# A mixture-of-experts tail: one scatter-add for the shared slot, an earlier bound of G, a later half of the second G

## The chip, the cores and the metric

The kernel runs on one core of a Trainium2 chip. The metric is the device time of one execution, in microseconds (us); several executions are run and their median is given. The engines' names are those of the profile: PE (TensorE matmul; PEld its weight loads), DVE (VectorE), ACT (ScalarE), POOL (GpSimd), SP (SyncE, which issues most DMAs). L789 means line 789 of the kernel before.

## The reference

Local-window attention feeds a soft mixture of experts, and that feeds a top-2 mixture of 8 experts. The change lies in the last part, of which this is the core:

```python
top2 = np.argpartition(-noisy_logits, 2, axis=1)[:, :2]
...
out = np.zeros((N, D), dtype=np.float32)          # N = 1536, D = 512, E = 8, F = 1024
for e in range(E):
    for k in range(2):
        mask = top2[:, k] == e
        h = np.maximum(x[mask] @ w1[e], 0.0)
        out[mask] += top2_w[mask, k, None] * (h @ w2[e])
```

Here `x` is the output of the soft mixture, `x = c @ slot_out`, with only 32 columns in `c`. So the kernel never forms `x`: for each expert it computes G = slot_out @ w1 once, and a row's `x @ w1` is its row of `c` times G.

## The kernel before

**Slots.** The 3072 (token, expert) pairs are sorted into slots of 128 rows: three slots for each expert (0 to 23), and one shared slot, number 24, that takes rows of up to four experts in four groups of 32. For slot n the kernel gathers the rows of `c` (`slot_a`, an indirect DMA issued by POOL, six slots ahead), transposes them (`slot_t`), computes h in 8 matmuls (`slot_h`; ACT writes the relu's high half, DVE the low half in `slot_l`), and then y in three times 8 matmuls of 512 columns (`slot_y`: high x high, high x low weight, low x high). ACT scales y into `ys`, and POOL adds the 128 rows to `out` in HBM with an indirect DMA that accumulates (`add_out`). Adds of one expert's three slots may overlap, since no token stands twice in them. Every other add waits until the adds before it have landed.

**Ranks.** Rank r is the preparation of expert r, laid out over the slots of the experts before it. Its steps are: `g_mm` (G into PSUM, tile `pg`), `w_abs` (ACT, maxima of w2), `w_scale_a` (L757, DVE: maximum of these into column 0 of `wx`), `g_scale_a` (L785, ACT: maximum of G into `gm`), `g_bound` (L789, DVE: a bound from `gm` into column 1 of `wx`), `scale_b` (two one-column spreads on PE, L722, one for each column of `wx`, then powers of two on DVE, `pow2`, L732 to L735), `g_hi`, `g_lo`, `w_hi`, `w_lo` (splits into two fp16 halves) and `g_put` (G to its place). In the kernel before `g_bound` is called inside `scale_b`.

**Order.** From L677 on, PE, DVE and ACT take their instructions in the order in which the program writes them, and POOL's adds and gathers are kept in order as well. The loop at L1363 writes a slot as: `do(n,"0")`, 8 matmuls of y(n), h(n+1), `do(n,"l")`, low half of h(n+1), transpose of n+2, `do(n,"a")`, 16 matmuls of y(n), `do(n,"p")`, ys(n), adds, `do(n,"b")`. A rank step at place k falls on slot (BASE[r]+k)/4, quarter "0", "a", "p" or "b" by the remainder. So step 3 of rank 2 falls on (2,"b") and step 5 on (3,"a"). The shared slot's own steps stand in the list `SHARE`.

**The shared slot's end.** One token can have both of its rows in slot 24. An indirect add with one row twice would lose one of them. So `tok` has two last columns, for the first and the second choice, `rows()` (L1178) makes two columns of row numbers from them, and `Shared.add` runs twice over the same `ys`, each time with the other choice's rows sent to padding rows behind the output.

**Start of this part.** K0 and K1 are ranks 0 and 1. `direct` (L1079) makes the first two transposed row tables by matmuls with one-hot matrices instead of gathers. At L1107 the first half of K1's G stands between the first `direct` and h of slot 0.

Of the kernel before, what the change touches and what calls it, by code (L numbers as in the profile page):

```python
# [8 lines left out]
F32 = mybir.dt.float32  # L9
F16 = mybir.dt.float16  # L10
# [9 lines left out]
NTOK = 1536  # L20
# [18 lines left out]
         (21, "a", "mm", 6), (21, "a", "mm", 7), (21, "a", "end"), (21, "p", "add", NOWN), (21, "p", "add", NSLOT)]  # L39
BASE = [0, 0, 8, 19, 30, 41, 51, 62]  # L40
# [16 lines left out]
def emit(tc, d, near=True, stop=None):  # L57
    nc = tc.nc
    es = ExitStack()
    with es:  # L60
# [14 lines left out]

        c32 = cst.tile([128, 393 + NSLOT], F32, name="c32")

        def cut32(a, n):
            return c32[:, a:a + n]

        ident, sel4, blkm, iof = cut32(0, 128), cut32(128, 128), cut32(256, 4), cut32(260, 32)
        padrow, ovth, below = cut32(292, 1), cut32(293, 72).rearrange("p (e k) -> p e k", e=8), cut32(365, 8)
        sltm, quarter, pads = cut32(373, NOV), cut32(391, 1), cut32(392, NSLOT + 1)
        out = d["out"]
# [653 lines left out]
        class Rank:  # L738
# [26 lines left out]
            def scale_b(self):  # L765
                self.g_bound()
                (self.sw, self.iw), (self.sg, self.ig) = pow2(self.wx, "w")
# [221 lines left out]
        class Shared:  # L989
# [22 lines left out]
            def h(self):  # L1012
                room = ring(2).bitcast(F16)
                self.hh = room[:, 0:2048].rearrange("p (a f r) -> p a f r", a=2, f=8)
                self.ys = room[:, 2048:3072].bitcast(F32)
                self.phs = []
                for q in range(2):
                    ph = ps_h.tile([128, 4, 128], F32, name="h")
                    for i in range(4):
                        f = 4 * q + i  # L1020
                        for g in range(4):
                            a = 32 * g
                            nc.tensor.matmul(ph[:, i, a:a + 32], self.gq[:, g, 128 * f:128 * f + 128], self.ct[:, a:a + 32],  # L1023
                                             start=True, stop=True)
                    nc.scalar.activation(self.hh[:, 0, 4 * q:4 * q + 4], ph, AF.Relu)
                    self.phs.append(ph)
                slot_l(self.hh, self.phs)
# [22 lines left out]

            def add(self, c):
                pool_q.indirect_dma_start(out=out, out_offset=bass.IndirectOffsetOnAxis(ap=sidx[:, c:c + 1], axis=0),
                                             in_=self.ys, in_offset=None, compute_op=ALU.add)
# [25 lines left out]
        def direct(z):  # L1079
            pct = pm_([128, 128])  # L1080
            for t in range(NT):
                nc.tensor.matmul(pct, c16[:, t].rearrange("p a s -> p (a s)"), z[t // 6][:, :, t % 6], start=(t == 0),
                                 stop=(t == NT - 1))
            return pct
# [21 lines left out]
        K0.w_hi(1)  # L1106
        K1.g_mm((0, 1))  # L1107
        h0 = slot_h(0, t0, scratch([128, 2, 8, 128], F16))
        pct1 = direct(z1)
        for q in range(2, 4):  # L1110
            K0.w_hi(q)
# [16 lines left out]
        gidx = cs2.tile([128, NSLOT], I32, name="gidx")  # L1128
        sidx = cs2.tile([128, NSLOT + 1], I32, name="sidx")
        adds, late, sent = [], [], []  # L1130
# [44 lines left out]
        og = scratch([128, 2, NSLOT, 24], F16)  # L1175
        tok, pad = scratch([128, NSLOT + 1], F32), scratch([128, NSLOT + 1], F32)

        def rows():  # L1178

            ttt(tok[:, NSLOT - 1:NSLOT], tok[:, NSLOT - 1:NSLOT], tok[:, NSLOT:], ALU.subtract)  # L1180
            nc.vector.scalar_tensor_tensor(pad, tok, 0.0, pads, ALU.is_equal, ALU.mult)
            nc.vector.scalar_tensor_tensor(sidx, tok, -1.0, pad, ALU.add, ALU.add)

# [57 lines left out]
        def rank_steps(r):  # L1241


            def k(place, nm, *a):
                j, q = divmod(BASE[r] + place, 4) if isinstance(place, int) else (OWN * r - 3 + int(place[0]), place[1])
                at(j, "0apb"[q] if isinstance(q, int) else q, lambda: getattr(raw[r], nm)(*a))
# [11 lines left out]
            if r == 1:  # L1258
                k("1l", "w_scale_b")
                k("1l", "g_put", 1)  # L1260
            else:
                for q in range(4):
                    k((-1, 0, 1, 1)[q], "w_abs", q)
                k(2, "w_scale_a")
                k(5, "scale_b")
                k(5, "g_hi")
# [49 lines left out]
        nc.vector.tensor_scalar(gidx, pls[:, 0:NSLOT], -1.0, 0.0, ALU.add, ALU.max)  # L1316
        nc.vector.tensor_copy(tok, pls)  # L1317
        K0.w_lo(0)
        next(y0)
# [37 lines left out]
        do(1, "p")  # L1357
        list(y1)
        rows()
        slot_a(AHEAD + 1)  # L1360
# [153 lines left out]
def host(inputs, near=True):  # L1514
# [10 lines left out]
    crel[:, 167:] = -8.0 * 2.0 ** -(2.0 * np.arange(4) + i[:, None] // 64 + 1)  # L1525
    c32 = np.zeros((128, 393 + NSLOT), f32)
    c32[:, 0:128] = np.eye(128)
# [8 lines left out]

    c32[:, 392:] = i[:, None] + NTOK + 1 + 128 * (np.arange(NSLOT + 1) % OWN)
    c16 = np.zeros((128, K16W), f16)
# [46 lines left out]
```

## Time and profile before

| what | us |
|---|---|
| median of 3 runs (lowest, highest) | 358.52 (357.67, 359.04) |
| the profiled execution | 358.8 |
| its span, first to last instruction | 357.0 |
| around the span | 1.8 |
| PE busy (share of the span) | 326.3 (91%) |
| DVE, ACT, POOL busy | 226.8, 210.4, 126.9 |

A row of the timeline gives start and duration in us, the engine, the line, the operation, output and inputs, shape and count, and in brackets how long the engine had been idle before it and what ended that. Several like instructions in a row are merged into one row with their count. The granted clock of TensorE is 1.00 at 2.4 GHz and 0.50 at 1.2 GHz.

### The profile page before, as it was taken

To read this page: it belongs to the slowest core of one execution; us is meant where nothing else is said; L and a number is where in the kernel's file an instruction comes from. 1 tells how busy PE (TensorE), PEld (TensorE's weight loads), DVE (VectorE), ACT (ScalarE), POOL (GpSimd) and SP (SyncE) were. 2 spreads that over 40 slices of the span, in tenths; PEclk is the share of its full clock that TensorE was granted. 3 is DMA by queue.
4 is the path that set the end of the run, shared out by engine and by line. 5 is a ranking of instruction groups with operands and counts; after the bars stand their busy time and mean duration, and the time that the engine had idled before them with its cause. 6 is when DMAs were issued, how large, how long until landed. Compare 5 with 4: busy or idle time off the path is not lost. (4 is left out here: it accounts for less than half of the span.)

```text
span 357.0 us, 7647 instructions
## 1 busy us (share of the span) xinstructions
PE 326.3 (91%) x2666; PEld 187.0 (52%) x2666; DVE 226.8 (64%) x856; ACT 210.4 (59%) x494; POOL 126.9 (36%) x184
## 2 busy tenths in 40 slices
PE   6999999999998999978989799999996999999950
PEld 3677876787775443434554345444443544554420
DVE  7797858778746300186979783879495667977100
ACT  4787765778652211196629676767785686476210
POOL 6365544446310001200442543355326142611350
PEclk9999999999999999998989899999999899999995
DMA  7998888898999999999989999995847443233352
GB/s 198 303 327 269 292 321 266 261 328 277 272 335 382 397 394 393 395 402 397 388 198 344 315 380 349 372 347 132 258 64 180 124 57 45 34 44 47 46 79 30
DMA packets 44876, 89.61 MB, mean 251 GB/s; under 512 B 3248, under 2 KB 11952, under 8 KB 44832
## 3 DMA queue, kind: packets, MB, share of 16 engines
q1 hardware_dynamic: 40352, 81.49, 65.6%
q0 software_dynamic: 4480, 7.57, 14.0%
q8 instruction: 23, 0.38, 0.4%
q14 instruction: 21, 0.17, 0.2%
HBM read 77.91 MB, written 11.14 MB: 249 GB/s over the span
## 5 line engine op out<-in xcount | busy, mean ns | idle before, releaser
L1143 PE MATMUL y<-w2hl,hh 128*128 128x512 f16 x552 | 128.8, 388 | 0.0
L1143 PEld LDWEIGHTS <-hh 128*128 128x128 f16 x552 | 53.1, 100 | 63.4 <-issue 7.8
L225 ACT ACTIVATE Tt<-Tt,nm 128x167 f32<-128x167 f32 x96 | 40.7, 426 | 21.4 <-DVE nm L223 17.4
L237 POOL TENSOR_TENSOR Pb<-Tt,r 128x318 f32<-128x318 f32 x48 | 34.5, 719 | 45.2 <-DVE r L233 16.3
L1074 DVE SCALAR_TENSOR_TENSOR hh<-h,hh 128x512 f16<-128x512 f32 x46 | 29.5, 684 | 23.2 <-ACT hh L1066 23.1
L1152 POOL DMA_INDIRECT out_y<-ys,sidx x16 | 26.0, 1622 | 47.3 <-ACT ys L1149 46.4
L217 PE MATMUL s<-kx,qd 128*128 128x167 f32 x192 | 36.7, 332 | 3.4 <-DVE kx L203 1.7
L684 POOL DMA_INDIRECT cT<-ctab,gidx x23 | 28.0, 1215 | 23.3 <-DVE w2hl L1317 16.6
L217 PEld LDWEIGHTS s<-kx,qd 128*128 128x128 f32 x192 | 30.8, 210 | 7.0 <-issue 3.5
L223 DVE CUSTOM_DVE_ANT_0 Tt<-s,bias 128x167 f32<-128x167 f32 x96 | 27.8, 323 | 6.5 <-PE s L217 3.9
L248 PE MATMUL pt<-c,Pb 128*128 128x128 f32 x176 | 28.9, 285 | 0.6 <-POOL Pb L237 0.6
L1066 ACT ACTIVATE hh<-h 128x512 f16<-128x512 f32 x46 | 24.8, 592 | 7.4 <-PE h L1065 6.8
L268 PE MATMUL px<-PT,vt 128*64 128x128 f32 x352 | 28.9, 285 | 0.0
L1152 POOL DMA_INDIRECT out_y<-c,sidx x8 | 13.9, 1742 | 40.4 <-ACT hh L1066 12.9
L248 PEld LDWEIGHTS pt<-c,Pb 128*128 128x128 f32 x176 | 18.9, 140 | 8.3 <-issue 4.5
L268 PEld LDWEIGHTS px<-PT,vt 128*64 128x64 f32 x352 | 18.3, 136 | 7.8 <-issue 4.3
L1149 ACT ACTIVATE ys<-y,gsc 128x512 f32<-128x512 f32 x16 | 10.9, 682 | 19.2 <-PE y L1143 19.2
L250 ACT ACTIVATE PT<-pt 128x512 f32<-128x512 f32 (+1 forms) x32 | 17.8, 558 | 4.8 <-PE pt L248 3.5
L773 DVE SCALAR_TENSOR_TENSOR w2hl<-w2hl,pmw 128x1024 f16<-128x1024 f32 x16 | 20.1, 1278 | 0.1
L773 DVE SCALAR_TENSOR_TENSOR w2hl<-w,pmw,w2hl 128x1024 f16<-128x1024 f32 x16 | 20.0, 1276 | 0.1
L750 ACT ACTIVATE w2hl<-w 128x1024 f16<-128x1024 f32 x16 | 16.8, 1049 | 4.1 <-DVE w2hl L773 2.9
L770 ACT ACTIVATE w2hl<-w,pmw 128x1024 f16<-128x1024 f32 x16 | 17.6, 1143 | 1.5 <-DVE pmw L734 1.5
(295 smaller groups left out, 513.9 us busy)
## 6 DMA issues: line engine op xcount, KB each, us to landing
w<-in_w1a SPq DMA_DIRECT2D x16, 512.0 KB, 6.9
w<-in_w2a SPq DMA_DIRECT2D x16, 512.0 KB, 6.4
w<-in_w1a SPq DMA_DIRECT2D x8, 1024.0 KB, 8.9
w<-in_w2a SPq DMA_DIRECT2D x8, 1024.0 KB, 11.8
w<-in_w1b SPq DMA_DIRECT2D x8, 1024.0 KB, 13.6
w<-in_w2b SPq DMA_DIRECT2D x8, 1024.0 KB, 9.3
w2hl<-in_w1b SPq DMA_DIRECT2D x8, 1024.0 KB, 17.3
w2hl<-in_w2b SPq DMA_DIRECT2D x8, 1024.0 KB, 17.4
```

The costliest lines, as they stand in the source:

```text
L217: nc.tensor.matmul(s[:, t, :], qv[:, p, t, :], kx[T % 2][:, p, t, :], start=True, stop=True)
L223: nc.vector.tensor_tensor_reduce(Tt[:, t], s[:, t], bias[:, p, v], -0.125, 1e30, ALU.add, ALU.min, nm[:, t:t + 1])
L225: nc.scalar.activation(Tt[:, t], Tt[:, t], AF.Exp, bias=nm[:, t:t + 1], scale=-1.0, accum_out=st[:, t:t + 1])
L237: nc.gpsimd.tensor_tensor(pv, Pu[:, :, 8:167], r.unsqueeze(2).to_broadcast([128, 2, 159]), ALU.mult)
L248: nc.tensor.transpose(pt[:, ch, t], Pn[:, t, 128 * ch:128 * ch + 128], ident)
L268: nc.tensor.matmul(px[64 * h:64 * h + 64, p, :], vv[:, c:c + 64], PT[:, ch, :, 64 * h:64 * h + 64], start=(ch == 0 or m == 0), stop=(ch == 1))
L684: return lambda *a, **k: tc.keep_in_program_order(getattr(nc.gpsimd, op)(*a, **k))
L773: nc.vector.scalar_tensor_tensor(w2hl[:, self.r, 1, 2 * q:2 * q + 2], self.quarter(q), self.sw, w2hl[:, self.r, 0, 2 * q:2 * q + 2], ALU.m ...
L1066: nc.scalar.activation(hh[:, 0, 4 * q:4 * q + 4], ph, AF.Relu)
L1074: nc.vector.scalar_tensor_tensor(hh[:, 1, 4 * q:4 * q + 4], phs[q], 0.0, hh[:, 0, 4 * q:4 * q + 4], ALU.max, ALU.subtract)
L1143: nc.tensor.matmul(py, hh[:, hx, f], w2hl[:, e, wx, f], start=(n == 0), stop=(n == 23))
L1152: a = nc.gpsimd.indirect_dma_start(out=out, out_offset=bass.IndirectOffsetOnAxis(ap=sidx[:, j:j + 1], axis=0), in_=ys, in_offset=None, com ...
```

## The change

1. **Shared slot.** `rows()` compares the tokens of the shared slot's rows with each other (`twin`, 128x128, by one matmul `pl_tok` that puts the transposed token numbers into PSUM and one DVE pass) and sends one row of each pair to padding. The new `Shared.sum` multiplies `ys` by `twin` in one fp32 matmul of 512 columns, so that each row holds the sum of its token's rows, and DVE copies the result. `Shared.add` runs once.
2. **G's bound.** `g_bound` leaves `scale_b` and becomes step 3 of ranks 2 to 7, two quarters before it.
3. **Second G.** `K1.g_mm((0, 1))` moves behind h of slot 0 and the second `direct`.

```diff
-         (21, "a", "mm", 6), (21, "a", "mm", 7), (21, "a", "end"), (21, "p", "add", NOWN), (21, "p", "add", NSLOT)]
+         (21, "a", "mm", 6), (21, "a", "mm", 7), (21, "a", "end"), (21, "p", "sum"), (21, "p", "add")]
...
             def scale_b(self):
-                self.g_bound()
                 (self.sw, self.iw), (self.sg, self.ig) = pow2(self.wx, "w")
...
-                self.ys = room[:, 2048:3072].bitcast(F32)
+                self.ys, self.total = (room[:, a:a + 1024].bitcast(F32) for a in (2048, 3072))
...
-            def add(self, c):
-                pool_q.indirect_dma_start(out=out, out_offset=bass.IndirectOffsetOnAxis(ap=sidx[:, c:c + 1], axis=0),
+            def sum(self):
+
+                pz = ps_g.tile([128, 512], F32, name="pg")
+                nc.tensor.matmul(pz, twin, self.ys, start=True, stop=True)
+                self.ys = self.total
+                nc.vector.tensor_copy(self.ys, pz)
+
+            def add(self):
+                pool_q.indirect_dma_start(out=out, out_offset=bass.IndirectOffsetOnAxis(ap=sidx[:, NOWN:NSLOT], axis=0),
...
-        K1.g_mm((0, 1))
         h0 = slot_h(0, t0, scratch([128, 2, 8, 128], F16))
         pct1 = direct(z1)
+        K1.g_mm((0, 1))
...
-            ttt(tok[:, NSLOT - 1:NSLOT], tok[:, NSLOT - 1:NSLOT], tok[:, NSLOT:], ALU.subtract)
-            nc.vector.scalar_tensor_tensor(pad, tok, 0.0, pads, ALU.is_equal, ALU.mult)
-            nc.vector.scalar_tensor_tensor(sidx, tok, -1.0, pad, ALU.add, ALU.add)
+            both = tok[:, NOWN:NSLOT]
+            nc.vector.tensor_scalar(twin, pl_tok, both, None, ALU.is_equal)
+            nc.vector.tensor_reduce(pad[:, 0:1], twin, AX.X, ALU.add)
+            nc.vector.scalar_tensor_tensor(pad[:, 0:1], pad[:, 0:1], 1.5, tok[:, NSLOT:], ALU.is_gt, ALU.mult)
+            ttt(both, both, pad[:, 0:1], ALU.subtract)
+            nc.vector.scalar_tensor_tensor(pad, tok[:, 0:NSLOT], 0.0, pads, ALU.is_equal, ALU.mult)
+            nc.vector.scalar_tensor_tensor(sidx, tok[:, 0:NSLOT], -1.0, pad, ALU.add, ALU.add)
...
                 k(2, "w_scale_a")
+                k(3, "g_bound")
                 k(5, "scale_b")
...
         nc.vector.tensor_copy(tok, pls)
+        nc.vector.tensor_copy(tok16, pls[:, NOWN:NSLOT])
...
+        pl_tok = pm_([128, 128])
+        nc.tensor.matmul(pl_tok, tok16.to_broadcast([128, 128]), id16, start=True, stop=True)
         rows()
```

Left out are the sizes of constants and of `sidx`, and the two new tiles.

The order on DVE in slots 2 and 3, where rank 2's scale is made (`wx` the two maxima, `gm` the maximum of G, `pmw` the powers of two), before:

```order
L757 TENSOR_REDUCE wx<-wm 128x1
L773 SCALAR_TENSOR_TENSOR w2hl<-w2hl,pmw 128x1024
L1137 TENSOR_TENSOR gsc<-gate,invs 128x1
L1074 SCALAR_TENSOR_TENSOR hh<-h,hh 128x512 x2
L983 COPY ct<-m 128x128
L789 TENSOR_SCALAR wx<-gm 128x1
L732 TENSOR_REDUCE pmw<-m 128x2
```

The same place with the change:

```order
L757 TENSOR_REDUCE wx<-wm 128x1
L788 TENSOR_SCALAR wx<-gm 128x1
L772 SCALAR_TENSOR_TENSOR w2hl<-w2hl,pmw 128x1024
L1143 TENSOR_TENSOR gsc<-gate,invs 128x1
L1080 SCALAR_TENSOR_TENSOR hh<-h,hh 128x512 x2
L982 COPY ct<-m 128x128
L732 TENSOR_REDUCE pmw<-m 128x2
```

The bound moved ahead of five instructions. In rank 5 it moves ahead of the four from `gsc` to `ct` in the same way. In ranks 3, 4, 6 and 7 the order on DVE stays as it was.

The end of DVE's queue, from the shared slot's scale (`gsc`) on, before:

```order
L1046 TENSOR_TENSOR shx<-shx,invs 128x8
L1047 TENSOR_REDUCE gsc<-shx 128x1
L1048 TENSOR_TENSOR gsc<-gsc,gate 128x1
L1137 TENSOR_TENSOR gsc<-gate,invs 128x1
L1074 SCALAR_TENSOR_TENSOR hh<-h,hh 128x512 x2
```

And with the change:

```order
L1045 TENSOR_TENSOR shx<-shx,invs 128x8
L1046 TENSOR_REDUCE gsc<-shx 128x1
L1047 TENSOR_TENSOR gsc<-gsc,gate 128x1
L1055 COPY w_4137<-pg 128x512
L1143 TENSOR_TENSOR gsc<-gate,invs 128x1
L1080 SCALAR_TENSOR_TENSOR hh<-h,hh 128x512 x2
```

The copy of the sum stands ahead of the scale of slot 22 and of the low half of h of slot 23. On PE the one matmul of the sum stands between the 16 last matmuls of y(21) and the 8 first of y(22).

The end of POOL's queue (`w_...` the shared slot's rows, `c_...` and `ys` those of slots 21 to 23), before:

```order
L1152 DMA out_y<-ys,sidx 1920x512 x2
L684 DMA out_y<-w_4130,sidx 1920x512 x2
L1152 DMA out_y<-c_4411,sidx 1920x512
L1152 DMA out_y<-ys,sidx 1920x512 x2
L1391 TENSOR_LOAD regs_2433
```

And with the change:

```order
L1158 DMA out_y<-ys,sidx 1920x512 x2
L684 DMA out_y<-w_4137,sidx 1920x512
L1158 DMA out_y<-c_4420,sidx 1920x512
L1158 DMA out_y<-ys,sidx 1920x512 x2
L1407 TENSOR_LOAD regs_2433
```

One of the two adds of the shared slot is gone.

## Rows read from the trace of the kernel before

**Rows 1.** The page, part 1: busy time and share of the span.

```profile
PE 326.3 (91%) x2666; PEld 187.0 (52%) x2666; DVE 226.8 (64%) x856; ACT 210.4 (59%) x494; POOL 126.9 (36%) x184
```

**Rows 2.** Waits of PE, 185 to 345 us: total, times, longest.

```profile
PE m L722 <- DVE wx L789: 3.6, 2, 2.5
PE m L722 <- DVE wx L757: 1.9, 1, 1.9
...
```

**Rows 3.** Timeline around rank 2's spread, slots 2 and 3.

```profile
192.51 5.34 PE L1143 MATMUL y<-w2hl,hh 128*128 128x512 f16 x24
...
198.09 0.16 DVE L757 TENSOR_REDUCE wx<-wm 128x1 bf16<-128x4 f32 x1 [0.92 <-ACT w2hl L750]
...
198.22 0.20 ACT L785 ACTIVATION_READ_ACCUMULATOR glo<-pg 128x1 f32 x1
...
198.31 0.23 PE L722 MATMUL m<-id_b,wx 128*128 128x128 bf16 x1
...
200.85 0.14 DVE L789 TENSOR_SCALAR wx<-gm 128x1 bf16<-128x1 f32 x1
...
201.05 0.23 PE L722 MATMUL m<-id_b,wx 128*128 128x128 bf16 x1 [2.51 <-DVE wx L789]
...
201.12 7.03 PE L1143 MATMUL y<-w2hl,hh 128*128 128x512 f16 x24
```

**Rows 4.** One stretch behind it: length, PE busy, granted clock, DMA share, GB/s.

```profile
202.00:203.00 1.00, 1.00 (x4) 0.50 1.13 307
```

**Rows 5.** Timeline of PE, both spreads of rank 5.

```profile
258.41 0.54 PE L722 MATMUL m<-id_b,wx 128*128 128x128 bf16 x2
```

**Rows 6.** Timeline of PE, spreads of rank 4 and of rank 6.

```profile
239.05 0.28 PE L722 MATMUL m<-id_b,wx 128*128 128x128 bf16 x2
...
275.46 0.23 PE L722 MATMUL m<-id_b,wx 128*128 128x128 bf16 x1 [1.05 <-DVE wx L789]
```

**Rows 7.** Timeline of the end: PE, ACT and POOL from slot 21 on.

```profile
329.59 5.35 PE L1143 MATMUL y<-w2hl,hh 128*128 128x512 f16 x24
...
331.10 1.55 POOL L684 DMA_INDIRECT out_y<-w,sidx  x1 [4.13 <-ACT w L1049]
...
336.19 1.55 POOL L684 DMA_INDIRECT out_y<-w,sidx  x1 [3.54 <-DMA out_y<-w,sidx]
...
341.78 1.55 POOL L1152 DMA_INDIRECT out_y<-c,sidx  x1 [4.04 <-issue]
...
344.11 0.69 ACT L1149 ACTIVATE ys<-y,gsc 128x512 f32<-128x512 f32 x1 [4.54 <-PE y L1143]
345.50 1.55 POOL L1152 DMA_INDIRECT out_y<-ys,sidx  x1 [0.30 <-issue]
```

**Rows 8.** DMA issues, us to landing: third gather, shared slot's second add, last add.

```profile
cT<-ctab,gidx POOLq DMA_INDIRECT x1, 3.4
...
out_y<-w,sidx POOLq DMA_INDIRECT x1, 4.8
...
out_y<-ys,sidx POOLq DMA_INDIRECT x1, 5.4
```

**Rows 9.** Timeline of PE: fp32 matmuls of 512 columns, four side by side.

```profile
137.30 1.92 PE L658 MATMUL y<-w,hT 128*32 128x512 f32 x16
```

**Rows 10.** Timeline at the start: K1's G, first and third gather, first gathered transpose.

```profile
164.30 1.93 PE L612 MATMUL pg<-w2hl,soT 128*32 128x256 f32 x16
...
174.02 2.03 POOL L684 DMA_INDIRECT cT<-ctab,gidx  x1 [16.65 <-DVE w2hl L1317]
...
178.53 0.94 POOL L684 DMA_INDIRECT cT<-ctab,gidx  x1 [0.22 <-issue]
...
181.63 0.23 PE L981 MATMUL m<-k,cT 128*128 128x128 f16 x1 [1.00 <-DMA cT<-ctab,gidx]
```

**Rows 11.** Two stretches at the start, columns as in rows 4.

```profile
164.00:167.00 3.00, 3.00 (x28) 0.50 1.07 407
...
168.00:174.00 6.00, 6.00 (x67) 1.00 1.03 395
```

More of the change, by code (lines that the diff above doesn't have):

```diff
@@ L73, in emit @@
         mid = pool("mid", 1, s_wa)
-        c32 = cst.tile([128, 393 + NSLOT], F32, name="c32")
+        c32 = cst.tile([128, 392 + NSLOT], F32, name="c32")
         def cut32(a, n):
@@ L82, in emit @@
         padrow, ovth, below = cut32(292, 1), cut32(293, 72).rearrange("p (e k) -> p e k", e=8), cut32(365, 8)
-        sltm, quarter, pads = cut32(373, NOV), cut32(391, 1), cut32(392, NSLOT + 1)
+        sltm, quarter, pads = cut32(373, NOV), cut32(391, 1), cut32(392, NSLOT)
         out = d["out"]
@@ L1128, in emit @@
         gidx = cs2.tile([128, NSLOT], I32, name="gidx")
-        sidx = cs2.tile([128, NSLOT + 1], I32, name="sidx")
+        sidx = cs2.tile([128, NSLOT], I32, name="sidx")
         adds, late, sent = [], [], []
@@ L1175, in emit @@
         og = scratch([128, 2, NSLOT, 24], F16)
-        tok, pad = scratch([128, NSLOT + 1], F32), scratch([128, NSLOT + 1], F32)
+        tok, pad = scratch([128, NSLOT + 1], F32), scratch([128, NSLOT], F32)
+        tok16 = scratch([128, 1], F16)
+        twin = cs2.tile([128, 128], F32, name="twin")
         def rows():
-            ttt(tok[:, NSLOT - 1:NSLOT], tok[:, NSLOT - 1:NSLOT], tok[:, NSLOT:], ALU.subtract)
-            nc.vector.scalar_tensor_tensor(pad, tok, 0.0, pads, ALU.is_equal, ALU.mult)
-            nc.vector.scalar_tensor_tensor(sidx, tok, -1.0, pad, ALU.add, ALU.add)
+            both = tok[:, NOWN:NSLOT]
[5 more added lines that the diff above has]
+            nc.vector.scalar_tensor_tensor(sidx, tok[:, 0:NSLOT], -1.0, pad, ALU.add, ALU.add)
         def groups():
@@ L1525, in host @@
     crel[:, 167:] = -8.0 * 2.0 ** -(2.0 * np.arange(4) + i[:, None] // 64 + 1)
-    c32 = np.zeros((128, 393 + NSLOT), f32)
+    c32 = np.zeros((128, 392 + NSLOT), f32)
     c32[:, 0:128] = np.eye(128)
@@ L1535, in host @@
     c32[:, 391] = i // 32 / 4
-    c32[:, 392:] = i[:, None] + NTOK + 1 + 128 * (np.arange(NSLOT + 1) % OWN)
+    c32[:, 392:] = i[:, None] + NTOK + 1 + 128 * (np.arange(NSLOT) % OWN)
     c16 = np.zeros((128, K16W), f16)
```

## The prediction

> **What bounds the kernel now.** The page's first part comes first: PE is busy 91% of the span, the next engine 64% [rows 1]. Where PE is that full, a gain must come out of PE's own waits, out of work taken from PE, or out of what follows PE's last matmul. So the second view is PE's waits through the slots [rows 2]. Two releasers hold nearly all of them: L789, the bound of G, with 3.6 us in 2 waits (ranks 2 and 6), and L757 with 1.9 us in one. The third view is the timeline at the longest of these waits [rows 3], the fourth the granted clock just behind it [rows 4]. The last is the timeline behind the last slots, where PE is done and POOL and the DMAs set the end [rows 7, 8].
>
> **Rank 2's bound (change 2).** PE makes the spread of column 0 at 198.31 and could make that of column 1 right behind it. It waits 2.51 us, until 201.05, because DVE makes the bound only at 200.85 [rows 3]. The data were there long before: ACT's read of the maximum of G ends at 198.22 + 0.20 = 198.42. What lay between on DVE is queue order: a `w_lo`, a scale, two low halves and a copy. With the change the bound is the next instruction after L757, so it starts at about 198.45. From the bound's start to the spread it is 0.20 us in the trace (200.85 to 201.05), so PE goes on at about 198.65 to 198.75. That gains 2.3 to 2.4 us; I take 2.3.
>
> What PE does next is 16 matmuls of y(3), whose low weights of the last quarter come from the `w_lo` that the bound now pushes back by some 0.3 to 0.4 us. They are needed only by the last two of the first 8 matmuls, about 1.3 us after the start at 5.34 / 24 = 0.22 us each, and a `w_lo` of about 1.3 us that starts near 198.6 is done by then. The low half of h(4) comes 0.4 us later on DVE and is needed some five microseconds later. So nothing new is late there, and I cost the push-back at 0. If that cover were gone, it would cost the 0.4.
>
> **The clock behind that wait.** The 24 matmuls after the wait take 7.03 us, and the 24 before it take 5.34 [rows 3]. At 202 to 203 PE is fully busy and the granted clock is 0.50, the 1.2 GHz level [rows 4]. The fall followed the idle of 2.51 us. With an idle of some 0.4 us in its place I expect the clock to stay at 2.4 GHz, which gives back 7.03 - 5.34 = 1.7 us. The bounds are 0 and 1.7, and I take 1.7, because what is left of the wait is nearer to the unbroken stretch than to the broken one.
> The Trainium skill (TensorE: Matmul & The Clock Gate, section "A second HAM failure mode: psum-queue depth-cycling") says that short idles between groups of matmuls, when they come often enough, also make the clock swing between its levels. By that the rest of the wait could still bring the fall, and this term would be 0. No row here shows a fall after one idle of 0.4 us in full work.
>
> **Rank 5's bound.** Here the wait is short: rank 5's two spreads take 0.54 us together [rows 5], against 0.28 in rank 4, where they don't wait [rows 6]. Moved ahead, the bound is ready in time: 0.2 us gained. In ranks 3, 4 and 7 PE doesn't wait at the spread, and in rank 6 DVE's order doesn't change, so the 1.05 us wait there stays [rows 6], and with it the 1.9 for L757 before it [rows 2].
>
> **Rows of the shared slot.** Three small DVE operations become six, two of them 128 columns wide, and there is one more cast and one matmul of 128 columns. ACT passes 128x512 in 0.69 us [rows 7], so two passes of a quarter of that and four small ones are under 1.2 us; I take 0.8 on DVE, behind slot 1. The cover is L757, before which DVE idles 0.92 us for ACT's `w_abs` [rows 3], and an idle before the low half of h(3). Without that cover up to 0.8 would go to the spread of rank 2. On POOL the first add waits for these row numbers and starts 0.8 later; behind it are the adds of slots 1 and 2 and the gather of slot 8, which PE needs several slots later. So this is 0. The one matmul on PE is about 0.1 us, ahead of the wait of rank 2, which takes it in.
>
> **The end (change 1).** The sum is one fp32 matmul of 512 columns. The nearest row is eight of these, side by side in two groups of four, in 16 records and 1.92 us, tail included [rows 9]: 0.86 to 0.96 a group, so 0.9 us on PE. It comes after the 16 matmuls of y(21), at 329.59 + 16/24 of 5.35 = 333.2 [rows 7], long after `ys` (POOL had it by 331.10), so PE does not wait. PE's last y comes 0.9 later, the rows of slot 23 at 344.11 + 0.69 + 0.9 = 345.7, and POOL can start the last add at about 345.95, with 0.25 us for the hand-over.
> Before, that add started at 345.50, with the rows ready at 344.80. It stood behind two others, because each of the shared slot's adds takes POOL to the landing of the one before: 331.10, 336.19, then 341.78 for slot 21 [rows 7]. Now the sum ends at 334.1, the copy (between 0.6 and 0.7, as ACT's pass) at 334.8, the one add starts at 335.0, slot 21 follows 5.1 to 5.6 later, at 340.1 to 340.6, slot 22 1.9 later at 342 to 342.5, and slot 23 no more waits for POOL. Its start is 0.45 later, but it lands alone: 4.8 us as the shared slot's add against 5.4 [rows 8], so 0.6 less. The term is +0.45 - 0.6 = -0.15. Its ends are +0.9 (PE's whole matmul on the path, nothing given back) and -0.6; I take -0.1.
>
> **The second G (change 3).** The 1.93 us of the first half of K1's G lie in a stretch at half clock [rows 10, 11]; at full clock it would take about 1.0. Behind the second `direct` it has the full clock, but h of slot 0 then waits some 0.4 for its transposed table, and `direct` falls into the slow stretch. So PE comes 0 to 0.4 earlier to the row numbers of the slots. Behind these POOL starts the first gather at 174.02, and PE then idles 1.00 us at 181.63 for it [rows 10]. The third gather, issued 4.5 us later, at 178.53, lands 3.4 later, at 181.9 [rows 8, 10], so the landing of the first is not set by its issue. Nothing is gained: 0, between -0.3 and +0.3, but for the third rival.
>
> **The sum.** -2.3 - 1.7 - 0.2 - 0.1 = -4.3 us. Against the profiled execution (span 357.0, 1.8 around, 358.8) this is 354.5; against the median of 358.52 it is 354.2. I say 354.3.
>
> Does PE's lead last from slot 3 to the end? From 201 to 272 PE has no wait of weight but these, so y and h just come earlier. ACT's waits there are for y, so ACT comes earlier too, and the maxima of the next ranks with it. At rank 6 PE waits 3 us for DVE, DVE for ACT. That chain begins with rank 5's powers of two, which follow rank 5's spread and so come earlier by the same amount.
>
> **The rivals.**
> *The clock falls anyway.* The wait shrinks, but the 1.7 us stays lost: 354.3 + 1.7 = 356.0. For it: the rest of the wait stands behind h, a transpose and two spreads, work with few columns. Against: 0.4 us is far less than 2.51. Chance 0.10.
> *The lead is eaten.* If ACT's or DVE's chain before rank 6 does not move with PE, or a weight load comes late, PE waits there that much longer. The 4.0 us of rank 2 are gone and 0.2 + 0.1 remain: 358.2. For it: the waits there are already 3 us. Against: the chain's head is released by PE itself. Chance 0.12.
> *Slower: the start stays slow.* The clock rose again at 167 after a stretch that was filled in good part by G's matmuls [rows 10, 11]. With G moved out, that stretch holds a wait of 0.4 and the one-hot `direct`. If the clock is not granted back there, the work of 168 to 174, 6.0 us at full clock [rows 11], takes up to 12. The gather is issued after it, so this is on the path: -4.3 + 6.0 = +1.7, 360.2. It decides for slower when the slow stretch costs over 4.3 us more than now. Against: h and the `direct` still fill PE. Chance 0.05.
> *More is gained.* Rank 6's wait shortens as well, or the tail lands earlier: 352.8. Chance 0.06.
>
> **How the numbers follow.** The forecast, 354.3 with its own range 353.3 to 355.3, has 0.67. To leave out no more than 2 in 10 the range takes in the first rival and part of the fourth: 353.2 to 357.0. A measurement of this kernel can tell about 0.5% from no change, 1.8 us, so faster is below 356.7: the forecast, the first and the fourth rival, 0.83, less a little for the errors of the first: 0.81. Same is the second rival and half of the third, 0.14. Slower is 0.05.
>
> **What would show it.** In the profile after: the bound at about 198.5 and PE's second spread within 0.5 us of the first in rank 2; 24 matmuls behind it in about 5.3 us and a granted clock of 1.00 there; rank 5's spreads in 0.28; rank 6's wait as before, but some 4.2 us earlier; one add of the shared slot, slot 21's add about 5 us behind it, and the last add of slot 23 right after its rows, landing in about 4.8. The prediction is wrong if the clock is low behind rank 2's spread, if rank 6's wait has grown by what rank 2's lost, or if the low clock of the start lasts beyond 168.

## The result, and the profile after

The changed kernel takes 357.74 us (median of 20 runs, 354.33 to 362.33). The kernel before, run beside it, takes 360.52 (20 runs, 357.67 to 364.05), some 2 us more than in the three runs shown at first, so the comparison goes by the ratio: **0.9895, 95% interval 0.9864 to 0.9927**. Of 358.52 that is 354.8 (353.6 to 355.9); predicted were 354.3, 353.2 to 357.0. A second comparison gave 0.9918 (0.9888 to 0.9947). The gain is real, 3 to 4 us, in both cases a little smaller than predicted. A ratio compares fast runs alone, those within 1.5% of the fastest of their kernel, which is why it differs from the ratio of the medians, and as the profile that came with the first comparison is of a slow run (span 359.2), "after" here is the profile of the second and the first is called the other profile of after.

The page, part 1, busy time and share of the span, after (before: [rows 1]):

```profile
span 354.2 us, 7657 instructions
...
PE 322.3 (91%) x2669; PEld 183.7 (52%) x2669; DVE 227.3 (64%) x861; ACT 210.1 (59%) x494; POOL 126.0 (36%) x183
```

PE does three matmuls more and is busy 4.0 us less: at half clock PE is busy longer for the same work, and most of this is half clock that is gone behind rank 2 and, in this profile, behind rank 6. PE's waits of 185 to 345 us after (before: [rows 2]), total, times, longest:

```profile
PE m L722 <- DVE wx L788: 2.8, 3, 1.2
PE m L722 <- DVE wx L757: 1.9, 1, 1.9
```

L788 is the bound of G (L789 before). Of its old two waits the longest, 2.5, is gone and the 1.05 of rank 6 is still there. The other two of the three are a 1.17 in rank 1, which lay ahead of this window before, and a 0.62 in rank 7. The 1.9 for L757 is untouched. The timeline around rank 2's spreads after (before: [rows 3]):

```profile
200.58 0.16 DVE L757 TENSOR_REDUCE wx<-wm 128x1 bf16<-128x4 f32 x1 [0.55 <-ACT w2hl L750]
...
200.71 0.20 ACT L784 ACTIVATION_READ_ACCUMULATOR glo<-pg 128x1 f32 x1
...
200.80 0.58 PE L722 MATMUL m<-id_b,wx 128*128 128x128 bf16 x2
...
200.94 0.16 DVE L788 TENSOR_SCALAR wx<-gm 128x1 bf16<-128x1 f32 x1 [0.20 <-ACT glo L784]
201.01 1.27 DVE L772 SCALAR_TENSOR_TENSOR w2hl<-w2hl,pmw 128x1024 f16<-128x1024 f32 x1
```

The bound now stands behind L757, waits 0.20 for ACT's read of the maximum, and the long `w_lo` comes behind it. PE starts y(3) at 201.22, 0.42 after the first spread, and has idled 0.13 of that; before it was 2.81 (198.31 to 201.12), with 2.51 idle. The stretch behind it, columns as in [rows 4], and behind it the spreads of rank 5 and of rank 6 (before: [rows 5, 6]):

```profile
202.00:203.00 1.00, 1.00 (x7) 1.00 1.07 317
```

```profile
256.83 0.27 PE L722 MATMUL m<-id_b,wx 128*128 128x128 bf16 x2
...
272.35 0.23 PE L722 MATMUL m<-id_b,wx 128*128 128x128 bf16 x1 [1.91 <-DVE wx L757]
273.62 0.23 PE L722 MATMUL m<-id_b,wx 128*128 128x128 bf16 x1 [1.05 <-DVE wx L788]
```

The clock is at 1.00, rank 5's spreads take 0.27, and rank 6's waits are those of before to 0.01 us. The end after, PE, DVE, POOL and ACT (before: [rows 7]), and then the landing of the last add (before: [rows 8]):

```profile
330.46 1.02 PE L1053 MATMUL pg<-w,twin 128*128 128x512 f32 x2
...
331.52 0.69 DVE L1055 COPY w<-pg 128x512 f32<-128x512 f32 x1 [4.83 <-PE pg L1053]
332.49 1.56 POOL L684 DMA_INDIRECT out_y<-w,sidx  x1 [8.12 <-DVE gsc L1143]
...
338.23 1.56 POOL L1158 DMA_INDIRECT out_y<-c,sidx  x1 [4.18 <-ACT ys L1155]
340.09 1.56 POOL L1158 DMA_INDIRECT out_y<-ys,sidx  x1 [0.30 <-issue]
342.38 0.69 ACT L1155 ACTIVATE ys<-y,gsc 128x512 f32<-128x512 f32 x1 [4.54 <-PE y L1149]
343.34 1.56 POOL L1158 DMA_INDIRECT out_y<-ys,sidx  x1 [1.69 <-ACT ys L1155]
```

```profile
out_y<-ys,sidx POOLq DMA_INDIRECT x1, 4.7
```

One add of the shared slot stands in the place of two, slot 21's add comes 5.74 behind it, and the last add waits for its own rows, 0.27 after they are ready. The landing takes 4.7 in place of 5.4.

### Where the time went

The span of one profile mixes these gains with a start that differs from run to run. So I cut it at PE's events: the spread of rank 0's maximum of W (the one that waits 1.13 us for L757; 162.08 before), the transpose of slot 2's gathered table (T2; 181.63 before, [rows 10]), PE's restart on y behind rank 2's spreads (201.12), rank 3's and rank 5's spreads (219.59 and 258.41), the last spread of rank 6 (275.46), the restart on y behind rank 7's (296.33 before), and the end of the span. Lengths in us, each worked out from these rows of PE's timeline:

| stretch | before | after | other profile of after | after - before | predicted |
|---|---|---|---|---|---|
| span start to rank 0's spread | 162.08 | 163.12 | 167.37 | +1.04 | 0 |
| to T2 | 19.55 | 20.28 | 20.30 | +0.73 | 0 |
| T2 to PE's restart in rank 2 | 19.49 | 17.82 | 17.75 | -1.67 | -2.3 |
| restart to rank 3's spreads | 18.47 | 16.79 | 16.79 | -1.68 | -1.7 |
| rank 3's to rank 5's spreads | 38.82 | 38.82 | 38.72 | 0.00 | 0 |
| rank 5's to the last of rank 6 | 17.05 | 16.79 | 16.81 | -0.26 | -0.2 |
| to the restart in rank 7 | 20.87 | 20.00 | 20.86 | -0.87 | 0 |
| to the end of the span | 60.67 | 60.58 | 60.60 | -0.09 | -0.1 |

Behind T2 the sum is -4.57 in the profile after and -3.84 in the other one, against -4.3 predicted. What lies ahead of T2 took some of it back.

### The profile page after: what moved, and what is told of

It is laid out like the page before. It is cut to its first block, busy times and chain, and to the rows that moved or that the text cites. A ratio compares the mean times of both kernels' runs of the same rounds, so it can differ in the third digit from the quotient of the medians.

```text
span 359.2 us, 7657 instructions
## 1 busy us (share of the span) xinstructions
PE 328.4 (91%) x2669; PEld 188.0 (52%) x2669; DVE 228.7 (64%) x861; ACT 210.0 (58%) x494; POOL 126.4 (35%) x183
## 4 chain that ended last, share of the span: by engine, by line
PE 60%; DMA 16%; DVE 10%; ACT 5%; issue 3%; POOL 2%; DVEq 1%; SPq 0%; POOLq 0%; ACTq 0%
PE y L1149 20%; PE s L217 8%; PE px L268 7%; PE pt L248 6%; DMA w<-in_w1a 4%; DMA w<-in_w2b 3%; PE pg L612 3%; DMA qd<-in_qt 3%; PE y L658 3%; PE h L612 2%; DMA w<-in_w1b 2%; DMA cT<-ctab,gidx 2%; PE h L1071 2%; DMA vt<-in_kv 2%; PE psl L301 2%
## 5 line engine op out<-in xcount | busy, mean ns | idle before, releaser
L237 POOL TENSOR_TENSOR Pb<-Tt,r 128x318 f32<-128x318 f32 x48 | 34.7, 722 | 50.5 <-DVE r L233 17.1
L217 PE MATMUL s<-kx,qd 128*128 128x167 f32 x192 | 37.5, 337 | 6.2 <-DMA qd<-in_qt 2.6
L217 PEld LDWEIGHTS s<-kx,qd 128*128 128x128 f32 x192 | 31.8, 215 | 9.0 <-issue 4.3
L248 PE MATMUL pt<-c,Pb 128*128 128x128 f32 x176 | 29.9, 292 | 0.3 <-POOL Pb L237 0.3
L268 PE MATMUL px<-PT,vt 128*64 128x128 f32 x352 | 29.7, 290 | 0.0
L248 PEld LDWEIGHTS pt<-c,Pb 128*128 128x128 f32 x176 | 19.2, 143 | 8.5 <-issue 6.7
L750 ACT ACTIVATE w2hl<-w 128x1024 f16<-128x1024 f32 x16 | 16.8, 1053 | 4.4 <-DVE w2hl L772 3.0
## 6 DMA issues: line engine op xcount, KB each, us to landing
w<-in_w1a SPq DMA_DIRECT2D x8, 1024.0 KB, 10.8
```

The costliest lines, as they stand in the source:

```text
L217: nc.tensor.matmul(s[:, t, :], qv[:, p, t, :], kx[T % 2][:, p, t, :], start=True, stop=True)
L237: nc.gpsimd.tensor_tensor(pv, Pu[:, :, 8:167], r.unsqueeze(2).to_broadcast([128, 2, 159]), ALU.mult)
L248: nc.tensor.transpose(pt[:, ch, t], Pn[:, t, 128 * ch:128 * ch + 128], ident)
L268: nc.tensor.matmul(px[64 * h:64 * h + 64, p, :], vv[:, c:c + 64], PT[:, ch, :, 64 * h:64 * h + 64], start=(ch == 0 or m == 0), stop=(ch == 1))
```

## The experiments

**The changed kernel again, and each of its parts alone.** Four kernels on one chip, beside one set of runs of the kernel before (median 360.2 of 29). The first has no edit.

> The changed kernel once more, for a profile of a run like the one shown of before, and for the ratio. My theory: ratio 0.988 (-4.3 of 358.5); in the profile rank 2's two spreads together in 0.28 us, the 24 matmuls behind them in 5.3 us at a granted clock of 1.00, rank 6's wait about 3 us as before, the last add landing in about 4.8. The rival that the lead is eaten: rank 6's wait at 7 us and a ratio of 0.999. The rival that the clock falls anyway: 7.0 us for the 24 matmuls and a ratio of 0.993.

Its ratio is 0.9918 (0.9888 to 0.9947); its profile is the one shown above.

The bound alone, on the kernel before:

```
             def scale_b(self):
-                self.g_bound()
...
+                k(3, "g_bound")
```

> The kernel before with the bound of G as step 3 of ranks 2 to 7 and nothing else of the change. My theory: this part carries nearly all of it, -2.3 (wait), -1.7 (clock), -0.2 (rank 5): -4.2 us, ratio 0.988, the same as the whole change. The rival that the sum of the shared slot brings it (one landing of 5 us less at the end): ratio near 1.000 here and 0.988 for the sum alone.

Measured: 0.9858 (0.9787 to 0.9929), span 353.9. Its rows at rank 2:

```profile
199.50 0.59 PE L722 MATMUL m<-id_b,wx 128*128 128x128 bf16 x2 [0.28 <-DVE wx L757]
...
199.93 0.59 PE L1142 MATMUL y<-w2hl,hh 128*128 128x512 f16 x2
```

From T2 (182.82 here) to PE's restart at 199.93 it is 17.11 us, 2.38 less than before, and the 24 matmuls behind take 5.34. The bound alone gives the whole gain.

The shared slot's sum alone: `rows`, `sum`, the one `add` and their constants as in the diff, `g_bound` and `K1.g_mm((0, 1))` in their old places.

> The kernel before with the one add of the shared slot (twin matrix, sum by one matmul, one indirect add) and nothing else. My theory: -0.1 us, between -0.6 and +0.9, so a ratio of 1.000; in the profile PE ends 0.9 us later against rank 6's spread than before, the last add starts right behind its rows and lands in 4.8 instead of 5.4. The rival: it takes a landing of some 5 us off the end, ratio 0.987.

Measured: 1.0025 (0.9994 to 1.0055), no change of time. At the end, from the start of the last add to the end of the span, it is 10.8 in place of 11.5: the last landing is shorter, but counted from PE's restart in rank 7 that add starts 0.44 later (49.61 against 49.17), which takes most of it back, much as predicted (-0.6 and +0.45). The profile has something else to show. PE's rows at rank 2:

```profile
201.57 0.22 PE L722 MATMUL m<-id_b,wx 128*128 128x128 bf16 x1
...
203.72 0.23 PE L722 MATMUL m<-id_b,wx 128*128 128x128 bf16 x1 [1.93 <-DVE wx L789]
```

```profile
204.00:206.00 2.00, 2.00 (x11) 1.00 1.08 317
```

The wait is 1.93, and the clock does not fall behind it. The wait is shorter because PE reached the first spread 1.0 us later, counted from T2: the clock had been low for longer behind rank 1.

The moved half of the second G alone:

```
-        K1.g_mm((0, 1))
         h0 = slot_h(0, t0, scratch([128, 2, 8, 128], F16))
         pct1 = direct(z1)
+        K1.g_mm((0, 1))
```

> The kernel before with the first half of the second G behind h of slot 0 and the second one-hot product, and nothing else. My theory: 0, between -0.3 and +0.3 us, ratio 1.000, the gather of slot 2 lands no earlier. The rival that the clock stays low at the start: the row numbers of the slots come up to 6 us later, ratio up to 1.017, and the granted clock is 0.50 where it was 1.00 before, during the second G and the first matmuls of y(0).

Measured: 1.0013 (0.997 to 1.0057), no change. Its wait at rank 2 and the stretches around it:

```profile
205.16 0.29 PE L722 MATMUL m<-id_b,wx 128*128 128x128 bf16 x1 [2.51 <-DVE wx L789]
```

```profile
204.00:205.00 1.00, 0.00 (x0) 0.56 1.09 264
205.00:206.00 1.00, 0.84 (x3) 0.50 1.14 277
```

After 2.51 us of idle (and 1.19 ahead of the first spread) the clock has gone to 0.50 while PE still waits, and the 24 matmuls take 8.16.

**Is it PE's idle that brings the fall?** The kernel before, with ten matmuls between the two spreads of rank 2, written into one more tile; the bound comes no earlier.

```
+                    if self.r == 2 and i == 0:
+                        fill = ph_([128, 512])
+                        for _ in range(10):
+                            nc.tensor.matmul(fill, warmw[:, 0:128], warmw[:, 0:512], start=True, stop=True)
```

> The kernel before, with ten matmuls of 128x512 added on PE between rank 2's two spreads; their product is used by nothing. The bound comes as late as before, so the second spread still starts about 2.5 us behind the first, but PE works in between. Theory (it is PE's idle of 2.5 us that takes the clock down): the 24 matmuls behind the spread take about 5.3 us in place of 7.0 to 8.2, the first spread of rank 2 to rank 3's spreads takes about 19.5 in place of 21.3, and the time is about 1.7 us lower than before (ratio about 0.995). Rival (the clock falls there whatever PE does, or the fall comes only in some runs): the 24 matmuls take 7 us or more here, or the time is that of before (ratio 0.998 to 1.003).

Rows at rank 2 (L773 is the added work):

```profile
199.56 2.32 PE L773 MATMUL h<-c 128*128 128x512 f16 x10
202.25 0.23 PE L769 MATMUL m<-id_b,wx 128*128 128x128 bf16 x1 [0.36 <-DVE wx L796]
202.31 5.34 PE L1150 MATMUL y<-w2hl,hh 128*128 128x512 f16 x24
```

PE restarts 2.81 behind the first spread, as before, and 19.49 behind T2, as before, but the clock holds: the first spread to rank 3's spreads is 19.60 in place of 21.28. So in this one profile the wait and the clock are two separate losses, as the prediction had them, and work without any use in the wait gives the second back. In time it gives no verdict: the ratio is 0.9899 (0.9835 to 0.9963), but the medians of all runs are alike (361.6 and 361.2).

**Rank 6, the wait that stays.** Between the maximum of W and the bound DVE loads the slots' row numbers into registers, and ahead of the maximum stands a `w_lo` of rank 5. DVE's rows before:

```profile
272.78 1.27 DVE L773 SCALAR_TENSOR_TENSOR w2hl<-w,pmw,w2hl 128x1024 f16<-128x1024 f32 x1
273.98 0.15 DVE L757 TENSOR_REDUCE wx<-wm 128x1 bf16<-128x4 f32 x1
275.25 0.16 DVE L789 TENSOR_SCALAR wx<-gm 128x1 bf16<-128x1 f32 x1 [1.12 <-issue]
```

The first kernel moves the loads, the second both, each in the changed kernel; the third does both with the bound alone.

```
-SHARE = [(6, "p", "groups"), (10, "b", "gather"), (13, "p", "regs"), ...
+SHARE = [(6, "p", "groups"), (10, "b", "gather"), (14, "a", "regs"), ...
...
-            k(12, "w_lo", 3)
+            k(14 if r == 5 else 12, "w_lo", 3)
```

> The changed kernel, with the loads of the slots' rows into registers (four in a row on DVE) one step later, out from between the maximum of W and the bound of rank 6. Theory (the 1.05 us wait of rank 6's second spread is these loads): the two spreads of rank 6 stand about 0.3 apart, rank 6's second spread comes 1.1 us earlier, and the time is 1.1 lower than the changed kernel's (about 0.989 of before; lower still where the clock behind rank 6 stays up). Rival (the lead is eaten by the next wait, as the prediction's second rival has it for rank 2): the spread comes earlier, but rank 7's spread waits that much longer, and the time is the changed kernel's, 0.992.

> As the run before, and the last low half of W of rank 5 two slots later on DVE, out of the way of rank 6's maximum of W. Theory (all 3 us that PE waits at rank 6 are DVE's queue): rank 6's first spread waits under 0.6 us, the two spreads stand 0.3 apart, the matmuls behind them run at 2.4 GHz, and the time is 2.3 to 4 us lower than the changed kernel's (0.981 to 0.986 of before). Rival (the first spread waits for ACT's part of the maximum, not for DVE's queue): its wait stays near 1.9 us and only the 1.1 of the second spread is gained.

> The kernel before with the bound of G moved ahead as in the change, and the two moves of the run before; the shared slot's sum and the second G stay as before. If the change's other two parts bring nothing, its time is that of the run before within 0.5 us. If the shared sum brings the 0.15 us that the prediction gives it, it is that much slower; if the moved half of G costs something at the start (rank 2's first spread came 1.7 us later, counted from rank 0's, in the changed kernel than before), it is up to 1.5 us faster.

Two of the four runs of the first kernel took 796 and 1080 us, at a clock of 1.00 and for a reason that no trace shows, so it has no ratio. Those of the other two kernels are 0.9900 (0.9800 to 0.9999) and 0.9874 (0.9778 to 0.9970), neither apart from the changed kernel's. The rows of rank 6 in the first kernel and in the second:

```profile
272.22 0.29 PE L722 MATMUL m<-id_b,wx 128*128 128x128 bf16 x2 [1.91 <-DVE wx L788]
```

```profile
271.37 0.29 PE L722 MATMUL m<-id_b,wx 128*128 128x128 bf16 x2 [0.71 <-DVE wx L788]
```

Rank 5's spreads to the last of rank 6 are 15.6 and 14.4 in place of 16.8, so both moves bring rank 6 forward, some 1.2 us each; of the first spread's wait 0.71 stays, a little more than expected. But the time does not follow, and PE's rows in the third kernel say where it goes (the last two are rank 7's spreads):

```profile
285.73 0.61 PE L1064 MATMUL h<-ct,Gst 128*128 128x128 f16 x8 [1.33 <-DVE ct L982]
...
289.68 0.22 PE L722 MATMUL m<-id_b,wx 128*128 128x128 bf16 x1
291.55 0.23 PE L722 MATMUL m<-id_b,wx 128*128 128x128 bf16 x1 [1.66 <-DVE wx L788]
```

The 2.4 us are spent on two new waits for DVE of 1.33 and 1.66. This is the second rival's mechanism, the lead eaten at the next rank, for another lead than the one it was written for.

**Rank 7's bound.** DVE's rows there, still in the third kernel, show the same order that rank 2 had: the bound (L788) behind two low halves of h and a copy.

```profile
289.17 0.16 DVE L757 TENSOR_REDUCE wx<-wm 128x1 bf16<-128x4 f32 x1 [2.30 <-ACT w2hl L750]
...
290.01 1.29 DVE L1073 SCALAR_TENSOR_TENSOR hh<-h,hh 128x512 f16<-128x512 f32 x2 [0.62 <-ACT hh L1065]
291.22 0.21 DVE L982 COPY ct<-m 128x128 f16<-128x128 f16 x1
291.35 0.15 DVE L788 TENSOR_SCALAR wx<-gm 128x1 bf16<-128x1 f32 x1
```

```
-                k(3, "g_bound")
+                k(2 if r == 7 else 3, "g_bound")
```

> The kernel with the moved bound and the two moves at rank 6, and with rank 7's bound one step further ahead, right behind the maximum of W. Theory (the gain of rank 6 was eaten at rank 7 by the same queue order: the bound stood behind the two low halves of h and a copy): rank 7's spreads stand 0.3 to 0.5 apart instead of 1.9, and the time is 1.4 us lower than without this move: about 0.980 to 0.984 of before. Rival (DVE itself is late at rank 7, by the low halves of W in front): PE's waits move to the h behind, and the time stays that of the run without.

Measured: **0.9848 (0.9789 to 0.9907)**, median 354.48, a little short of what was expected. PE's rows at rank 7:

```profile
286.47 0.61 PE L1064 MATMUL h<-ct,Gst 128*128 128x128 f16 x8 [1.33 <-DVE ct L982]
...
290.43 0.29 PE L722 MATMUL m<-id_b,wx 128*128 128x128 bf16 x2
```

The spreads stand together. From T2 to the end it is 169.96, against 170.80 and 171.53 in the two profiles of after. It has the lowest ratio here, but that it is faster than the bound alone or the changed kernel is not shown: the intervals overlap. From rank 5's spreads to the end it takes 97.0 us; the ten profiles with the old order at rank 6 take 97.9 to 98.6 where the clock fell behind rank 6 and 96.7 to 98.4 where it held. Part of the gain goes on to the next h, which now waits 1.21 (at 299.58) for DVE. The chain of work that ended last runs over ACT and DVE from 288.85 up to that h, and mostly over PE behind it.

**The bound alone once more, and with the sum.** No edit in the first; the second is the changed kernel with `K1.g_mm((0, 1))` in its old place.

> The kernel with the moved bound alone once more, for more runs. Theory (the bound is the whole gain): 0.984 to 0.990 of before. Rival (its first six runs were a lucky draw): 0.991 to 0.994, as the changed kernel's. In the trace the restart of PE behind rank 2's spreads comes 17.1 us after T of slot 2 (before 19.5), or up to 1.1 more where the clock is low between the spreads of rank 1 and y(2).

> The changed kernel with the second G back in its old place: the bound and the shared sum alone. If the moved half of G costs something (from rank 0's spread of the maximum of W to T of slot 2 the kernels with it moved take 19.2 to 20.3, those without 19.1 to 20.3: means 20.0 and 19.5), this kernel is some 0.5 us faster than the changed one and takes 19.1 to 19.6 there. If it costs nothing, the two are alike within 0.5 us and that stretch scatters as before. The cost of the row numbers on DVE, if any is left, shows as PE's restart behind rank 2's spreads later than 17.1 us after T of slot 2.

Measured: 0.9886 (0.9819 to 0.9953) and 0.9885 (0.9821 to 0.9948). The first is in the theory's range, and all these kernels lie within each other's intervals: the sum and the moved G add nothing that can be measured to the bound. From rank 0's spread to T2 the two take 18.89 and 18.23, less than any kernel with the moved G. In the second, PE's restart in rank 2 comes 18.27 behind T2, later than 17.1, but not for the row numbers: T2 came early, and rank 1's bound, which stands ahead of them on DVE, made PE wait 1.62 there in place of 0.45.

**What the moved G does at the start.** PE's rows behind rank 0's spread, after (before: [rows 10, 11]), and the clock there:

```profile
165.79 0.85 PE L1071 MATMUL h<-ct,Gst 128*128 128x128 f16 x8 [0.38 <-DVE ct L1094]
166.43 2.25 PE L1088 MATMUL m<-w2hl,c 128*128 128x128 f16 x12
168.60 1.93 PE L612 MATMUL pg<-w2hl,soT 128*32 128x256 f32 x16
```

```profile
164.00:166.00 2.00, 1.62 (x13) 1.00 1.05 389
166.00:168.00 2.00, 2.00 (x18) 0.50 1.05 401
168.00:170.00 2.00, 2.00 (x20) 0.50 1.03 405
170.00:172.00 2.00, 2.00 (x18) 0.50 1.02 403
172.00:174.00 2.00, 2.00 (x21) 0.79 1.02 389
```

The half of G still takes 1.93: the slow stretch came later with it, and in this profile it is twice as long as before. The second `direct` takes 2.25 in it, hardly more than the first at full clock (2.22, at 163.19), so it is G to which half clock costs something. With G moved the clock falls here in all five profiles up to then, without the move in three of eight, and rank 0's spread to T2 has a mean of 20.0 with it (19.24 to 20.30) and 19.2 without (18.23 to 20.31). The new wait of 0.38 was my suspect, so the last kernel fills it:

```
+        fill = ph_([128, 512])
+        for _ in range(2):
+            nc.tensor.matmul(fill, warmw[:, 0:128], warmw[:, 0:512], start=True, stop=True)
         h0 = slot_h(0, t0, scratch([128, 2, 8, 128], F16))
```

> The changed kernel with two matmuls of 128x512 added on PE (about 0.44 us; their product is used by nothing) in the place where h of slot 0 now waits 0.38 us for its transposed table. In the five profiles with the moved half of G the granted clock falls to 0.50 some 3 to 5 us behind rank 0's spread of the maximum of W each time, and in three of the eight without the move. Theory (the short wait before h of slot 0, new with the move, brings the fall): the clock stays at 1.00 through the 12 us behind that spread, and T of slot 2 comes about 19.0 behind it, in place of 19.8 to 20.3. Rival (the wait has nothing to do with it; what counts is that the heavy matmuls of G no longer stand there, or it is chance): the clock is at 0.50 there for 3 us or more again, and T comes 19.8 or later. In time the difference is at most 1 us of 357, about what the comparison can resolve.

```profile
163.94 0.23 PE L722 MATMUL m<-id_b,wx 128*128 128x128 bf16 x1 [1.13 <-DVE wx L757]
...
169.91 1.07 PE L612 MATMUL pg<-w2hl,soT 128*32 128x256 f32 x16
```

```profile
164.00:166.00 2.00, 2.00 (x13) 0.87 1.04 383
166.00:168.00 2.00, 2.00 (x14) 0.50 1.05 396
168.00:170.00 2.00, 2.00 (x16) 0.77 1.03 410
```

The wait is filled, PE is busy from rank 0's spread on, and the clock falls all the same, for 3 us; T2 comes 19.91 behind that spread. My theory that this wait brings the fall does not hold. The fall comes 1.6 us behind the spread here, as in the profile before, against some 3 to 4.5 us in the five with the wait, so the half of G now lies behind it and takes 1.07. Ahead of the fall stands another idle, the 1.13 us that PE waits at rank 0's spread in all fourteen profiles; no run takes it away, so whether it brings the fall is not tested. In time the kernel is at 0.9867 (0.9815 to 0.9920), no different from the changed one. Six falls of six with the move and three of eight without may be the move's doing or chance, and that stays open.

T2 is a rough mark for this, since in all profiles but one PE waits there, up to 1.93 us, for the first gather to land. POOL's start of that gather shows PE's own delay better. Counted from rank 0's spread it comes at 10.7 in the five profiles where the clock held, all without the move; at 11.8 to 12.0 in the three without the move where it fell (before: 11.94, [rows 10]) and with the filled wait; at 12.2 to 12.5 in four with the move; and at 13.4 in the profile after, where the low clock lasted twice as long. So a fall costs some 1.2 us here, the move adds up to 0.5, and filling the wait gave the 0.5 back.

## Why the prediction was right, point by point

- **Rank 2's wait, -2.3: right.** In the profiles whose clock agrees from T2 on (before and the bound alone) it is 19.49 to 17.11, -2.38. In the profile after it is -1.67, because rank 1's bound made PE wait 1.17 there in place of 0.45. The other profile's -1.74 holds 1.08 us that PE lost to a low clock between rank 1's spreads and y(2); the bound alone, which changes nothing in that stretch, lost it in its second profile too (17.74). In the changed kernel the full gain shows only in the version with the filled wait (17.09).
- **The clock behind it, -1.7: right against this profile of before, too simple as a rule.** The restart to rank 3's spreads took 16.79 in all ten profiles with the moved bound, so the rival that the rest of the wait still brings the fall did not come true: 0 to 0.6 us of idle stayed there. By the rule of the Trainium skill that the prediction weighed (TensorE: Matmul & The Clock Gate, section "A second HAM failure mode: psum-queue depth-cycling") short idles bring the clock down when they come often enough. Here 0 to 0.6 us at this place did not, ten times of ten. But the loss that is taken away is not the same in each run: 1.7 before, 2.8 with G alone, none with the sum alone after 1.93 us of idle.
- **Rank 5, -0.2: right.** From rank 5's spreads to the last of rank 6, 16.78 to 16.85 in six profiles with the bound moved and DVE's order at rank 6 unchanged and 17.05 to 17.13 in four without.
- **The lead lasts: right for this change.** Rank 3's to rank 5's spreads are 38.82 before and after, and rank 6's waits are the same 1.91 and 1.05. The rival that eats it came true only for the moves at rank 6.
- **Rows of the shared slot, 0: right.** The six operations on DVE take 1.40 us in place of 0.51 (0.9 more; 0.8 estimated), and PE's restart comes no later for it: 17.09 us behind T2 with them (the kernel with the filled wait) and 17.11 without. The cover held as predicted: L757 follows rank 1's first spread by 15.8 us with them and without (198.09 - 182.31 before, 200.58 - 184.80 after).
- **The end, -0.1: right, by its parts.** The fp32 matmul took 1.02 (0.9 predicted), the copy 0.69, slot 21's add came 5.74 after the shared one (5.1 to 5.6), the last landing took 4.7 in place of 5.4. From rank 7's restart to the end it is -0.09, which one pair of profiles hardly resolves; in time the sum alone is worth nothing that can be measured.
- **The second G, 0: not shown to be wrong, but wrong in its picture.** I had G escape into the fast stretch and `direct` fall into the slow one. In five profiles of six the slow stretch moved along; with the wait filled it came as I had it. The third rival, that the start stays slow, is there in small in one: 6.8 us at half clock in the profile after (the stretches above, summed), against little more than the 3 of [rows 11] before; in the other five with the move it was no longer than before. What it costs, 0.8 us in the means to T2, can't be told from the scatter in time. It is about the size by which the two comparisons missed 354.3 (354.8 and, by 0.9918, 355.6).
- **Not in the sum:** rank 6's clock. With the same waits of 1.91 and 1.05 the clock fell behind them in six of ten profiles, and the stretch to rank 7 took 20.4 to 20.8 in these and 19.1 in the others. That is 1.4 to 1.7 us of luck in any single profile, before and after. The -0.87 of the table is of this kind: the clock held, and 0.62 of what that gave went into a wait at rank 7 that was not there before. Without it the sum behind T2 is -3.7, near the -3.84 of the other profile.

## What to carry to other kernels

When an engine that is busy 91% of the time waits for one small operation, look at what stands ahead of that operation on its own engine; moving it ahead of longer ones that are needed only later was worth all of this change's 1%, and the two other parts were worth nothing that could be measured. Ask at once where the same order stands again: at rank 6 and 7 it did, and a lead gained ahead of it is spent there. Cut a profile at events of the busiest engine and compare the pieces, since whole spans differ by more than the change is worth.

## What was not expected of the hardware

- The start took 162.08 to 167.37 us to rank 0's spread in the profiles here, before anything that the change touches. That is more than the whole gain. In the six profiles that show no fall of the clock in it, it took 162.08 to 163.67; in the eight others 162.09 to 167.37.
- The same idle of PE does not always bring the same clock. About 3 us of it in two pieces at rank 6 was followed by a fall in six of ten profiles; 1.91 to 1.93 us in one piece was not, in two of two; 2.51 was, in two of two. At rank 1, where PE idles 1.4 to 2.4 us for the gather and for the bound (1.00 and 0.45 before), a fall followed in thirteen of fourteen, with the change and without. What decides it is not shown. None of the changes here takes this loss away.
- Four loads of row numbers into registers, which do no work on data, held up the bound behind them in DVE's queue for over 1 us: without them PE's wait of 1.05 was gone.
